# The first three units' y is copied into x by partitions, with the rows of x and w_in in that order; the first v is reversed by a product; some loads begin later

## The chip, the core and the metric

The kernel runs on one core of a Trainium2 chip. The core has five engines that run side by side and meet at semaphores: TensorE (matrix products into PSUM), VectorE (DVE), ScalarE (ACT), GpSimd (POOL) and SyncE (SP), whose queue here does nothing but issue transfers. Transfers between HBM and SBUF, and within SBUF, run on 16 DMA engines that all queues share.

The metric is the device time of one execution in microseconds (us). The time before is a median of 599.5 us over 3 runs (599.27 to 601.45).

## The reference

Two parts are computed one after the other. The first is a recurrence over 768 tokens with a 48 x 48 state per batch and head (4 batches, 8 heads):

```python
f = 1.0 / (1.0 + np.exp(-f_logit))
for t in range(S):
    state = f[:, :, t, :, None] * state + np.einsum('bhd,bhe->bhde', k[:, :, t], v[:, :, t])
    y[:, :, t] = np.einsum('bhd,bhde->bhe', q[:, :, t], state)
```

The second takes y with the heads side by side as x (3072 tokens of 384 values), and is a small network with 2048 hidden values:

```python
h = x @ w_in
g = h * (1.0 / (1.0 + np.exp(-1.702 * h)))
return g @ w_out
```

q, k, v and f_logit arrive as float32. The weights w_in (384 x 2048) and w_out (2048 x 384) arrive as float64 bits, so the kernel turns them into float32 itself.

## The kernel before

**Units.** The 3072 tokens are cut into 12 units of 256. A unit has two halves of 128 tokens (f = 1 is the first, kept in order; f = 0 the second, kept in reversed order), and each half two groups (g) of 64. Eight heads form four pairs (NP); head h of a pair (h = 0 or 1) lies on partitions 64h to 64h+47 (the function `rows`). So of each 64 partitions only 48 hold data.

**The recurrence of a unit** is done in levels. `begin_f`, `begin` and `begin_k` bring the decays F, the queries and the keys to the layout with head dimension on partitions (line 345, or for the first three units, n < N_FILL = 3, products with an identity, line 357, copied out by ScalarE at line 362). `begin_gates` (line 407) multiplies neighbouring decays on POOL into the tile `tot`, level by level (line 413); there is one such tile, so the next unit's gates wait until the last reader of this unit's is done, which is the state update (line 664). Each of six levels l has score products (line 422, `sc`), a `promote` on the DVE that multiplies X by decays (line 516 for the first three units, line 520 for the others), a `set_aside` that copies keys into Kc on ScalarE (line 491) and `evacuate`, which moves the scores under masks into the tile A (lines 463 and 482 on the DVE, 472 on ScalarE). `turn_k` turns the keys (`tkn`, line 592, copied into kn at line 593). The part "S" then makes the products kn with v (`pd`, line 640), `add` makes y from A and v (line 531), and the states st are updated (lines 661 to 665). The last part adds the share of earlier states to y (line 686).

**v** is loaded per unit in two tiles (`load_v`): vt holds the first 128 tokens as they are, vr the second 128 in four transfers of 32 tokens each, in reversed order of the four. `reverse_v` (line 309) turns each 32 rows round by a shuffle on the DVE, so that all 128 stand reversed in vt.

**From y to x.** y lies in PSUM with head dimension on partitions. Eight ScalarE copies per unit (line 698; each of one h, f and g, 48 partitions x 4 pairs x 64 tokens) bring it to the tile yT in SBUF. The function `to_x` then builds xT by transfers: x has 384 rows in three chunks (NK = 3) of 128. Rows 0 to 95 of chunk c are the pair of heads 2c and 2c+1, packed without a gap; rows 96 to 127 of the three chunks together hold the fourth pair. So a unit has two transfers of 48 x 768 (line 737) and four smaller ones of 32 or 16 rows (line 742). w_in is loaded with its rows in the same order, each pair of 128-column blocks as two pieces, 96 and 32 partitions (line 210).

**The network.** h = x w_in is line 1084 for the first four units and o = g w_out line 1098 for the first three; after that the two use schemes with fewer products of smaller blocks, whose operands are sums made on POOL (`sums_of_x`, line 952) and on the DVE. Lines 990 and 853 are their products.

**What sets the order.** For TensorE and POOL the order is that in which the program is written out, everywhere. For the first four units (`opening` and the first `merge` calls, inside `fill_order`) this holds for all engines. After that DVE, ACT and SP are ordered by a planner that goes by estimated times. `opening` is unit 0 with the beginnings of unit 1; `merge` deals the network's products (the list `fill`) between the parts of a unit's recurrence. Weights are fetched by `fetch_weights`, one pair of blocks at a time, three pairs in flight, and turned to float32 by `convert`: one ScalarE operation (line 228) and four DVE operations (lines 230 to 233).

PSUM tiles of the first units come from `bank`, which hands out four lanes in turn, or those in the list `chosen`. A product into a lane waits until the earlier tile there has been read. On SP each transfer waits for the transfer eight places before it, since the program has eight counters for them.

In `opening` unit 0's parts that matter here stand in this order: scores of level 5, the last gelu table, `turn_k`, the copies of the scores into A with v's reversal between them, the queries of unit 1, then part "S" with the keys of unit 1 between pd and y. There, `begin_k` of unit 1 ends with the set-aside copy Kc, and only then come y's products and a 1 x 1 copy of y by ScalarE (`seen`, line 651), for which the next products into y wait.

Of the kernel before, what the change touches and what calls it, by code (L numbers as in the profile page):

```python
# [9 lines left out]
F32 = mybir.dt.float32  # L10
# [3 lines left out]
ALU = mybir.AluOpType  # L14
# [9 lines left out]
def kernel(  # L24
# [137 lines left out]

    q_end = const.tile([P, NP], F32, name="q_end")
# [7 lines left out]
    D2, DR = 2 * D, P - 2 * D  # L171
    assert NP == NK + 1 and NK * DR == D2
# [5 lines left out]
    for r in range(NGR):  # L178
        ffs = range(r * FG, (r + 1) * FG)
        for ff in ffs[::2]:  # L180
            f = slice(ff * P, (ff + 2) * P)
            pairs.append((w_in[:, :, f], [
                (lambda t: t[:D2], moe_w_in[0:NK * D2, f].rearrange("(c p) f -> p c f", c=NK)),
                (lambda t: t[D2:], moe_w_in[NK * D2:DM, f].rearrange("(c p) f -> p c f", c=NK)),
            ]))
        for ff in ffs[::2]:
            pairs.append((w_out[:, ff:ff + 2, :], [
                (lambda t: t[:], moe_w_out[ff * P:(ff + 2) * P, :].rearrange("(c p) f -> p c f", c=2))]))
# [100 lines left out]
    def load_v(n):  # L289


        if n >= NALL:
            return
        b, s0 = n // NU, n % NU * U
        vts[n] = ld.tile([P, 2, DM], F32, tag="vt", name=f"vt_{n}", bufs=2)
        vrs[n] = ld.tile([P, DM], F32, tag="vr", name=f"vr_{n}", bufs=1)
        nc.sync.dma_start(
            out=vts[n][:, 1].rearrange("p (h d) -> p h d", h=H), in_=v[b, :, s0:s0 + HALF, :].rearrange("h p d -> p h d")
        )
        for i in range(4):  # L300
            t0 = s0 + U - 32 * (i + 1)
            nc.sync.dma_start(
                out=vrs[n][32 * i:32 * (i + 1)].rearrange("p (h d) -> p h d", h=H),
                in_=v[b, :, t0:t0 + 32, :].rearrange("h p d -> p h d"),
            )

    def reverse_v(n):

        nc.vector.stream_shuffle(vts[n][:, 0], vrs[n], list(range(31, -1, -1)))
# [9 lines left out]
    def attention(n):  # L319
# [58 lines left out]
        def begin_f(pieces=None):  # L378
# [7 lines left out]
            if n >= N_FILL or (n == 1 and R - 4 in pieces):  # L386
                load_raw(n + 1, 0)
# [6 lines left out]
        def begin_k(between=None):  # L394
# [9 lines left out]
            else:  # L404
                set_aside(0)

        def begin_gates():
            t["tot"], off = att.tile([P, NA], F32, tag="tot", name=f"tot_{n}"), 0
            for m in LEV:
                nb = NA // (2 * m)  # L410
                t2 = t["tms"][-1].rearrange("p (n two) -> p n two", two=2)
                tn = t["tot"][:, off:off + nb]
                nc.gpsimd.tensor_tensor(tn, t2[:, :, 0], t2[:, :, 1], ALU.mult)  # L413
# [214 lines left out]
        def _():  # L628
# [17 lines left out]
            if not n:  # L646
                units[1][0][2]()
                add()

                seen = t["py"][HS:HS + 1, 1, 0, 1, :1]  # L650
                nc.scalar.copy(seen, seen)
            load_v(n + 1)
            st = att.tile([P, NC, NP, D], F32, tag="st", name=f"st_{n}", bufs=2)
# [15 lines left out]
        def _():  # L669
# [22 lines left out]
            if width(n) > U:  # L692
                nc.gpsimd.memset(xT[:, :, U + 1:], 0.0)
            def half(h):
                for f in (1, 0):
# [37 lines left out]
        def to_x(y, x, ng, hs=range(2)):  # L733

            for h in hs:
                most, rest = y(h)
                nc.sync.dma_start(out=x[h * D:(h + 1) * D].rearrange("p c (g t) -> p c g t", g=ng), in_=most)
                at = 0
                while at < D:
                    c, p = (h * D + at) // DR, (h * D + at) % DR  # L740
                    w = min(D - at, DR - p)
                    nc.sync.dma_start(
                        out=x[D2 + p:D2 + p + w, c].rearrange("p (g t) -> p g t", g=ng), in_=rest(h * HS + at, w)
                    )
                    at += w
# [508 lines left out]
    def opening():  # L1254
# [17 lines left out]
        fetch_weights()  # L1272
# [12 lines left out]
        chosen[:] = [2, 3]  # L1285
        turn_k(0)
        turn_k(2)
        for l in range(NL - 1):
            evacuate(l)
            if l == 1:  # L1290
                units[0][3]()
# [64 lines left out]
```

## Time and profile before

| | |
|---|---|
| median of 3 runs | 599.5 us |
| the profiled execution | 599.04 us |
| its span, first to last instruction | 596.9 us |
| mean granted TensorE clock | 0.994 |
| TensorE busy (products) | 574.9 us, 96% |
| VectorE busy | 431.5 us, 72% |
| ScalarE busy | 291.8 us, 49% |
| GpSimd busy | 138.1 us, 23% |
| the eight yT copies of all units (line 698) | 96 copies, 35.3 us |
| transfers yT to xT | 24 of 144 KB, 24 of 32 KB, 24 of 16 KB |

In the page's lists, PE is TensorE's products, PEld its weight loads, which overlap them. A product in float32 appears as two passes, so the counts of the trace are twice those of the program. A row of the timeline gives start, busy time, engine, line, operation and tiles, and in brackets how long the engine had been idle before it and what ended that. A row of the chain of waits gives start, duration and what the time went to; "issue" is time in which an engine waited for nothing that the profile shows. A row of a table of stretches gives the stretch, its length, the busy times of PE, PEld, DVE, ACT and POOL with their instructions, the granted TensorE clock, the share of the DMA engines' time and GB/s.

The span falls into three stages: up to some 75 us units 0 and 1 are begun while the weights arrive; from there to about 560 us recurrence and network are interleaved; the last 37 us finish the last unit.

### The profile page before, as it was taken

To read this page: it belongs to the slowest core of one execution; us is meant where nothing else is said; L and a number is where in the kernel's file an instruction comes from. 1 tells how busy PE (TensorE), PEld (TensorE's weight loads), DVE (VectorE), ACT (ScalarE), POOL (GpSimd) and SP (SyncE) were. 2 spreads that over 40 slices of the span, in tenths; PEclk is the share of its full clock that TensorE was granted. 3 is DMA by queue.
4 is the path that set the end of the run, shared out by engine and by line. 5 is a ranking of instruction groups with operands and counts; after the bars stand their busy time and mean duration, and the time that the engine had idled before them with its cause. 6 is when DMAs were issued, how large, how long until landed. Compare 5 with 4: busy or idle time off the path is not lost.

```text
span 596.9 us, 18468 instructions
## 1 busy us (share of the span) xinstructions
PE 574.9 (96%) x7814; PEld 513.7 (86%) x7814; DVE 431.5 (72%) x696; ACT 291.8 (49%) x613; POOL 138.1 (23%) x214
## 2 busy tenths in 40 slices
PE   6868899999999999999999999999999999999897
PEld 6756776867768789999999999999999999999897
DVE  2898986974866857889777888786887786361284
ACT  4746633453334352574574574573663564552440
POOL 3031200240027216412602502502502503303000
PEclk9979999999999999999999999999999999999999
DMA  7947857950242552353552343552361211001000
GB/s 187 208 124 176 195 143 192 238 110 1 52 106 65 141 136 64 78 132 82 130 147 43 88 113 82 139 133 61 97 158 42 63 37 29 27 3 27 28 1 26
DMA packets 83314, 58.29 MB, mean 98 GB/s; under 512 B 33633, under 2 KB 75265, under 8 KB 83233
## 3 DMA queue, kind: packets, MB, share of 16 engines
q1 hardware_dynamic: 82896, 56.73, 38.5%
q8 instruction: 61, 1.00, 0.7%
q10 hardware_dynamic: 337, 0.39, 0.3%
q14 instruction: 20, 0.16, 0.1%
HBM read 43.98 MB, written 8.39 MB: 88 GB/s over the span
## 4 chain that ended last, share of the span: by engine, by line
PE 76%; DVE 11%; ACT 6%; issue 3%; POOL 2%; DMA 2%; SPq 0%; DVEq 0%; ACTq 0%; POOLq 0%
PE h L990 15%; PE h L1084 13%; PE o_Y L853 9%; PE o L1098 9%; PE o_Z L853 7%; PE h_y L990 6%; PE sc L422 5%; PE o_X L853 3%; PE o_W L853 3%; ACT yT L698 2%; POOL tot L413 2%; PE y L531 1%; PE y L686 1%; DVE g L1018 1%; PE t L357 1%
## 5 line engine op out<-in xcount | busy, mean ns | idle before, releaser
L1084 PE MATMUL h<-xT,w_in 128*128 128x256 f32 x384 | 89.2, 387 | 2.0 <-DMA xT<-yT 1.9
L1084 PEld LDWEIGHTS h<-xT,w_in 128*128 128x128 f32 x384 | 72.7, 193 | 13.9 <-DMA xT<-yT 2.0
L491 ACT COPY Kc<-X 128x512 f32<-128x512 f32 x72 | 48.4, 672 | 72.3 <-DVE X L520 57.5
L520 DVE TENSOR_TENSOR X<-X,tot 128x1024 f32<-128x1024 f32 x45 | 57.5, 1278 | 32.2 <-PE sc L422 22.7
L1098 PE MATMUL o<-w_out,g 128*128 128x384 f32 x192 | 65.5, 491 | 0.4 <-DVE w_out L233 0.4
L413 POOL TENSOR_TENSOR tot<-F 128x512 f32<-128x512 f32 x12 | 12.5, 1041 | 204.5 <-DVE st L664 198.3
L1098 PEld LDWEIGHTS o<-w_out,g 128*128 128x128 f32 x192 | 35.4, 190 | 22.7 <-DVE w_out L233 0.9
L990 PE MATMUL h<-E,w_in 128*128 128x128 f32 (+1 forms) x420 | 53.4, 275 | 0.0
L853 PE MATMUL o_Y<-T,S 128*128 128x192 f32 x288 | 50.6, 329 | 0.0
L990 PEld LDWEIGHTS h<-E,w_in 128*128 128x128 f32 x420 | 50.1, 192 | 0.0
L1020 ACT ACTIVATE g<-g 128x512 f32<-128x512 f32 (+1 forms) x63 | 35.7, 585 | 25.7 <-DVE g L1018 25.2
L1088 ACT ACTIVATE g<-h 128x256 f32<-128x256 f32 x64 | 23.9, 383 | 48.5 <-PE h L1084 48.0
L853 PEld LDWEIGHTS o_Y<-T,S 128*128 128x128 f32 x288 | 46.8, 190 | 0.5
L698 ACT COPY yT<-y 48x256 f32<-48x256 f32 x96 | 35.3, 368 | 21.6 <-PE y L686 20.5
L482 DVE COPY_PREDICATED A<-masks,sc 128x256 f32<-128x256 uint32 (+1 forms) x98 | 42.0, 506 | 0.1
L1018 DVE TENSOR_TENSOR g<-g,h 128x512 f32<-128x512 f32 (+1 forms) x52 | 31.8, 632 | 12.6 <-PE h L990 11.5
L345 DVE STREAM_TRANSPOSE X<-raw 128x512 f32<-128x512 f32 x36 | 38.1, 1107 | 0.1
L372 POOL TENSOR_SCALAR F<-F 128x1024 f32<-128x1024 f32 x10 | 15.2, 1522 | 95.5 <-ACT F L375 83.8
L952 POOL TENSOR_TENSOR E<-xT 128x128 f32<-128x128 f32 (+1 forms) x32 | 19.4, 616 | 73.9 <-DMA xT<-yT 33.5
L422 PEld LDWEIGHTS sc<-X,Kc 48*64 48x64 f32 x1440 | 26.3, 136 | 11.1 <-issue 4.7
L422 PE MATMUL sc<-X,Kc 48*64 48x64 f32 x1440 | 31.1, 222 | 4.8 <-DVE s L230 1.3
L1018 DVE TENSOR_TENSOR g<-g,h_y 128x512 f32<-128x512 f32 (+1 forms) x26 | 16.5, 634 | 21.9 <-PE h_y L990 19.7
(159 smaller groups left out, 1169.3 us busy)
## 6 DMA issues: line engine op xcount, KB each, us to landing
bits<-in_moe_w_out_dram SPq DMA_DIRECT2D x8, 768.0 KB, 7.0
raw<-in_f_logit_dram SPq DMA_DIRECT2D x48, 96.0 KB, 3.1
raw<-in_k_dram SPq DMA_DIRECT2D x48, 96.0 KB, 3.3
bits<-in_moe_w_in_dram SPq DMA_DIRECT2D x8, 576.0 KB
raw<-in_q_dram SPq DMA_DIRECT2D x44, 96.0 KB, 2.3
k_tok<-z SPq DMA_DIRECT2D x56, 64.0 KB, 1.8
kt<-k_tok SPq DMA_DIRECT2D x14, 256.0 KB, 3.2
xT<-yT SPq DMA_DIRECT2D x24, 144.0 KB, 2.9
```

The lines of the kernel that those rows point to most:

```text
L345: nc.vector.transpose(view(out, at, [[HALF, NP], [step, R4], [R4 * step, 32]]), by_half[:, j, f].rearrange("p a (j d) -> p (a j) d", j=R4) ...
L422: nc.tensor.matmul(t["sc"][h][g * HS:(g + 1) * HS, a, s, :], lhsT=t["Kc", l][rows(h), x:x + HS], rhs=rhs(h, a, g), start=True, stop=True,)
L482: moved = nc.vector.copy_predicated(out=view(A, c * HALF + at, dims), mask=mask.bitcast(U32), data=got)
L491: nc.scalar.copy(c.rearrange("p (n two m) -> p n two m", two=2, m=m), view(X, KF * SLOT, [[2 * m, SLOT // (2 * m)], [(KR - KF) * SLOT + m, ...
L520: nc.vector.tensor_tensor(x, x, y, ALU.mult)
L698: nc.scalar.copy(view(yT[rows(h)], at, [[U, NP], [step, HS]]), py[columns(h, g), g, :, f, :])
L853: nc.tensor.matmul(t[name], lhsT=lhs(f), rhs=rhs(f), start=(new and i == 0), stop=(i == HF - 1), skip_group_check=True,)
L990: nc.tensor.matmul(ph[:, t], lhsT=WA[a][:, f * P:(f + 1) * P], rhs=E[n][b], start=(root and t == 0), stop=not goes_on, skip_group_check=True,)
L1018: nc.vector.tensor_tensor(to, to, part, ALU.add if sign > 0 else ALU.subtract)
L1020: nc.scalar.activation(to, to, AF.Gelu_apprx_sigmoid)
L1084: nc.tensor.matmul(ph, lhsT=w_in[:, c, ff * P:(ff + 1) * P], rhs=xTs[n][:, c, :], start=(c == 0), stop=(c == NK - 1))
L1098: nc.tensor.matmul(t["po"], lhsT=g[ff // FG][:, ff % FG, tt * P:(tt + 1) * P], rhs=w_out[:, ff, :], start=(ff == ffs[0]), stop=(ff == ffs[ ...
```

## The change

1. **Rows of x and w_in.** Chunk c of x now has head 2c+h on partitions 64h to 64h+47, exactly where y has it, and partitions 64h+48 to 64h+63 hold 16 rows of the fourth pair. w_in's pieces follow: four per pair of blocks (two of 48, two of 16 partitions) instead of two.
2. **y straight into x** for units 0, 1 and 2: for each h, four ScalarE copies of 48 x 64 bring the fourth pair to yT, from where three transfers of 16 rows each build the rest of x, and four copies of 48 x 192 write the three other pairs from PSUM into xT. In unit 0 the small copies and transfers of both h come before all the larger copies. From unit 3 on, the copies to yT stay as they were, and a unit has two transfers of 48 x 768 and six of 16 rows.
3. **The first v** is loaded in natural order in one transfer, and turned round by a product with a reversed identity (`turned`, made on POOL), which ScalarE copies to vt. It stands before `turn_k` in TensorE's order; the shuffle of unit 0 is gone.
4. **Loads**: the third `fetch_weights` (w_out's first pair) and the load of unit 2's f move from before unit 0's levels and from its level 3 to part "S" of unit 0, behind the loads of unit 1's v.
5. In part "S" of unit 0, y's products and the 1 x 1 copy now stand before the set-aside copy Kc of unit 1.
6. From unit 5 on, the last level of the gates goes into a tile of its own, with two buffers, instead of into `tot`.

```diff
+    turned = const.tile([P, P], F32, name="turned")
+    nc.gpsimd.memset(turned, 0.0)
+    nc.gpsimd.affine_select(
+        out=turned, in_=turned, compare_op=ALU.not_equal, fill=1.0, base=1 - P, pattern=[[1, P]], channel_multiplier=1
+    )
...
-    D2, DR = 2 * D, P - 2 * D
+    D2, DR = 2 * D, HS - D
...
-                (lambda t: t[:D2], moe_w_in[0:NK * D2, f].rearrange("(c p) f -> p c f", c=NK)),
-                (lambda t: t[D2:], moe_w_in[NK * D2:DM, f].rearrange("(c p) f -> p c f", c=NK)),
+                (lambda t, h=h: t[h * HS:h * HS + D], moe_w_in[0:NK * D2, f].rearrange("(c h p) f -> h p c f", c=NK, h=2)[h])
+                for h in range(2)
+            ] + [
+                (lambda t, h=h: t[h * HS + D:(h + 1) * HS],
+                 moe_w_in[NK * D2:DM, f].rearrange("(h c p) f -> h p c f", c=NK, h=2)[h])
+                for h in range(2)
...
+        if n == 0:
+            nc.sync.dma_start(
+                out=vrs[n].rearrange("p (h d) -> p h d", h=H), in_=v[b, :, s0 + HALF:s0 + U, :].rearrange("h p d -> p h d")
+            )
+            return
...
+        if n == 0:
+            pt = bank([P, DM], f"v_{n}")
+            nc.tensor.matmul(pt, lhsT=turned, rhs=vrs[n], start=True, stop=True)
+            nc.scalar.copy(vts[n][:, 0], pt)
+            return
         nc.vector.stream_shuffle(vts[n][:, 0], vrs[n], list(range(31, -1, -1)))
...
-            if n >= N_FILL or (n == 1 and R - 4 in pieces):
+            if n >= N_FILL:
                 load_raw(n + 1, 0)
...
             else:
+                if between:
+                    between()
                 set_aside(0)
...
+                if m == LEV[-1] and n > N_FILL + 1:
+                    tn = att.tile([P, nb], F32, tag="D64", name=f"D64_{n}", bufs=2)
                 nc.gpsimd.tensor_tensor(tn, t2[:, :, 0], t2[:, :, 1], ALU.mult)
...
             if not n:
-                units[1][0][2]()
-                add()
-
-                seen = t["py"][HS:HS + 1, 1, 0, 1, :1]
-                nc.scalar.copy(seen, seen)
+                def values():
+                    add()
+
+                    seen = t["py"][HS:HS + 1, 1, 0, 1, :1]
+                    nc.scalar.copy(seen, seen)
+                units[1][0][2](values)
             load_v(n + 1)
+            if not n:
+                fetch_weights()
+                load_raw(2, 0)
...
+            def copies(h, to, heads):
+                for f in (1, 0):
+                    for g in range(NG):
+                        at, step = (g * HS, 1) if f else (U - 1 - g * HS, -1)
+                        nc.scalar.copy(
+                            view(to, at, [[U, heads.stop - heads.start], [step, HS]]), py[columns(h, g), g, heads, f, :]
+                        )
+
             def half(h):
+                if n < N_FILL:
+                    copies(h, yT[rows(h), NK:], slice(NK, NP))
+                    to_x(lambda h: (None, lambda r, d: yT[r:r + d, NK]), xT[:, :, :U], NG, (h,))
+                    if n == 0 and h == 0:
+                        return
+                    for x in (0, 1) if n == 0 else (h,):
+                        copies(x, xT[rows(x)], slice(0, NK))
+                    return
...
-                nc.sync.dma_start(out=x[h * D:(h + 1) * D].rearrange("p c (g t) -> p c g t", g=ng), in_=most)
-                at = 0
-                while at < D:
-                    c, p = (h * D + at) // DR, (h * D + at) % DR
-                    w = min(D - at, DR - p)
+                if most is not None:
+                    nc.sync.dma_start(out=x[rows(h)].rearrange("p c (g t) -> p c g t", g=ng), in_=most)
+                for c in range(NK):
                     nc.sync.dma_start(
-                        out=x[D2 + p:D2 + p + w, c].rearrange("p (g t) -> p g t", g=ng), in_=rest(h * HS + at, w)
+                        out=x[h * HS + D:(h + 1) * HS, c].rearrange("p (g t) -> p g t", g=ng),
+                        in_=rest(h * HS + c * DR, DR),
                     )
-                    at += w
...
         load_raw(1, 1)
         fetch_weights()
-        fetch_weights()
...
-        chosen[:] = [2, 3]
+        chosen[:] = [2, 3, 2]
+        units[0][3]()
         turn_k(0)
         turn_k(2)
         for l in range(NL - 1):
             evacuate(l)
-            if l == 1:
-                units[0][3]()
```

More of the change, by code (lines that the diff above doesn't have):

```diff
@@ L170 @@
     k_toks = [tc.dram_tile([2, G, P // 32, 32 * NP], F32, name=f"k_tok{j}") for j in range(2)]
[L171 to L172 removed]
+    D2, DR = 2 * D, HS - D
+    assert NP == NK + 1 and NK * DR == D
     NGR = NFF // FG
```

## The prediction

> **What bounds the kernel now.** I read the page's busy times and slices first, then the stretches, then inside the first 130 us the waits of TensorE, the chain of waits and the timeline.
>
> ```profile
> PE 574.9 (96%) x7814; PEld 513.7 (86%) x7814; DVE 431.5 (72%) x696; ACT 291.8 (49%) x613; POOL 138.1 (23%) x214
> PE   6868899999999999999999999999999999999897
> ```
> ```profile
> 70.00:80.00 10.00, 9.39 (x118) 6.62 (x119) 9.86 (x16) 6.14 (x14) 4.75 (x6) 1.00 0.66 132
> 200.00:300.00 100.00, 99.25 (x1374) 92.81 (x1374) 78.79 (x117) 50.39 (x105) 34.98 (x45) 1.00 0.43 107
> 300.00:400.00 100.00, 99.73 (x1428) 97.14 (x1428) 78.71 (x121) 57.03 (x110) 22.68 (x38) 1.00 0.43 107
> ```
>
> The columns of a stretch are its length, then PE, PEld, DVE, ACT, POOL busy. From 200 to 400 us TensorE is idle for 1.0 us: work moved there on another engine can win next to nothing. From 75 to 125 us it is busy for all of 50.0 us. So what counts is when TensorE gets through the first 75 us, and every delay there is carried to the end. Three places in it matter. First the timeline of unit 0 from 22 us:
>
> ```profile
> 21.96 1.09 PE L592 MATMUL tkn<-ident,X 128*128 128x128 f32 x8
> 22.66 1.07 ACT L593 COPY kn<-tkn 128x512 f32<-128x512 f32 x2
> 23.29 1.97 PE L357 MATMUL t<-ident,raw 128*64 128x128 f32 x32 [0.24 <-ACT kn L593]
> 24.47 0.70 DVE L309 STREAM_SHUFFLE vt<-vr 128x384 f32<-128x384 f32 x1
> 27.17 1.51 ACT L472 COPY A<-sc 32x256 f32<-32x256 f32 x4 [0.39 <-DVE A L482]
> 30.07 1.10 PE L531 MATMUL y<-A,vt 64*48 64x64 f32 x62 [1.59 <-ACT X L362]
> ```
>
> The shuffle sits between the DVE's copies into A, but ScalarE waits only 0.39 us for them; the run of ScalarE (kn, X, a, A, X) is almost as long, and TensorE's y waits for its end. Second, the chain of waits at x of unit 0 and at unit 1:
>
> ```profile
> 35.68 0.45 ACT Kc L491
> 36.12 3.26 DMA xT<-yT
> 39.38 0.04 issue
> 39.43 4.39 PE h L1084 x12
> ...
> 73.63 0.36 ACT yT L698
> 73.99 0.02 issue
> 74.02 0.69 ACT Kc L491
> 74.71 0.04 issue
> 74.75 0.70 PE sc L422 x32
> ```
>
> Unit 0's h waits for the transfer yT to xT; unit 1's does not: there the eight yT copies and the Kc copy behind them hold the scores, so copies are the price, not transfers. Third, the clock (the number behind POOL's busy time):
>
> ```profile
> 36.00:37.00 1.00, 0.57 (x20) 0.57 (x24) 0.96 (x2) 0.38 (x1) 0.00 (x0) 0.50 0.32 74
> 41.00:42.00 1.00, 1.00 (x4) 0.82 (x3) 0.86 (x3) 0.00 (x0) 0.00 (x0) 0.50 1.01 390
> 42.00:43.00 1.00, 1.00 (x4) 0.78 (x4) 0.97 (x2) 0.38 (x1) 0.00 (x0) 0.72 1.00 389
> ```
>
> Unit 0's first twelve h matmuls take 4.39 us against 2.86 us for twelve at 71.76: they begin at half clock, which lasts until some 42.6 us.
>
> **The change, part by part.** Times are those of the profiled execution, 599.04 us (span 596.9 and 2.1 around it); the median of the runs shown, 599.5, is 0.46 above it.
>
> *First v by a product.* Gone: 0.70 us of DVE. Added: one fp32 product of 384 columns, two passes of 0.34 (sixteen such o passes take 5.43), so 0.68 us on TensorE ahead of tkn, and a ScalarE copy 128x384 of 0.475 (the sum<-o row, 2.9 for 6) ahead of kn. The second tkn takes the product's bank and waits for that copy. tkn_0 starts at 22.64, the v copy ends about 23.3, tkn_2 runs 23.4 to 24.0, its copy ends 24.65, and t, now in that bank, starts at 24.8 instead of 23.29: +1.5. ScalarE's X, a and A copies follow, less the 0.39 us for which they waited for the DVE: +1.1, and y with them, at 31.2. Bounds: if y is let go by the A copies, not by X, it starts at 29.6 (-0.5); if nothing of the 0.39 comes back, +1.5. I take +1.1, since the 1.59 us row names X. pd moves from 25.19 to 26.7, the state updates behind it by about 0.9, and the DVE's weight conversions likewise; the DVE sits idle for 2.37 us before 46.41, which swallows that.
>
> *seen ahead of Kc.* Kc ended (30.80) before y did (31.19), so nothing was held. Now Kc ends about 0.4 us before the yT copies can start. No gain, no cost.
>
> *y straight into x, unit 0.* Before: 8 copies of 256, 0.38 us apart, and six transfers issued 0.6 us apart from 34.15, the last at 37.33, landing about 39.4, which is 6.9 us after y's end at 32.54. Now 8 copies of 64 and 8 of 192. ScalarE's PSUM copies cost 0.31 at 192 elements, 0.475 at 384: 0.21 at 64. Transfers start after four small copies (0.9), go out every 0.6 with nothing to wait for, the last at 3.9, landing 2.1 later: 6.0 after y's end. But the sixteen copies take 8x0.21 + 8x0.315 = 4.2 instead of 3.04, Kc takes 0.7 more, and the scores of unit 1 (1.13 at half clock) stand ahead of h in TensorE's order: h at 6.25. So h starts at 32.54 + 1.1 + 6.25 = 39.9, +0.47. Until 42.68 it runs at half rate (2.78 us do 1.39 of 2.86), so it ends at 44.15 instead of 43.82: **+0.3**. Ends: -2.2 (h at 38.8 and never cooled) and +2.1 (cold 3.4 us longer).
>
> *The same for unit 1.* Sixteen copies again, 4.2 against 3.04, ahead of Kc. TensorE had finished its h at 74.62 and already waited, so the scores at 74.75 move by **+1.15**, and behind 75 us nothing gives it back. Ends: 0.4 (copies of 64 at 0.12, as the 1x1 copy) to 1.4. The transfers themselves are needed only at 80.65 (h of unit 1); they land about 79.
>
> *Unit 2.* Four copies (1.51) become eight (2.1) ahead of a Kc that waited 0.44 us for the DVE anyway, and the scores that read it stand behind TensorE's o: 0.
>
> *Loads.* On SP, v's reversed load is one issue instead of four (2.06 to 0.5) and q of unit 1 goes out 1.5 us sooner; nobody waited. The second v load now waits for the product (22.7) instead of the shuffle (25.2). Behind it stand w_out's first pair (19.12 to about 24.8, read at 39.20), f of unit 2 (19.85 to 25.2, read at 43.75) and x: covers of 7, 14 and 9 us less 5 to landing. w_in's pieces go from two to four: 16 more issues of 0.45 us. At the start they fit before f's load, for which SP waits until 8.70. The tight place is the pair issued at 41.12 and read at 51.59: its last piece goes out at 42.9 and lands 7.8 us later, 50.7. Cost 0 to 2, taken 0. From unit 3 on x takes eight transfers instead of six: 1.2 us on SP; TensorE waits for none of these transfers behind 100 us.
>
> *POOL.* The matrix for the product: a memset and a select of 0.20 and 0.29 (ident's rows) at 3.2 us; POOL's next work is at 9.45. The last gates in a tile of their own: tot waits for the state updates 198 us in all, but no TensorE wait names POOL. 0; the orders planned for DVE, ACT and SP shift with it, and with 1.3 us of TensorE idle in 300 that is +-1.
>
> Sum +0.3 + 1.15 = +1.45: 600.5 for a profile, **601.0 us** as a median.
>
> *A rule against the change.* The row first: the two pieces of that w_in pair are issued 0.42 us apart and overlap. The Trainium skill, page "DMA: Bandwidth & Descriptors", section "Rules for kernel authors", advises one 128-partition transfer over pieces by partitions, and gives a fixed cost of about 2.0 us each. By it two further pieces, paid one after the other, would be an estimated 4 us and the sum would be 605; by the row they are 0.9 us of issue, hidden.
>
> **The rivals.**
>
> *Longer cold (slower).* Half clock lasted from about 35.8 to 42.6, some 6.8 us, over two gaps of TensorE. If the 3.4 us before its usual end holds too little work because h starts at 39.9 or later, another 3.4 us at half clock follow: the h take 5.7 us and t and scores half more, +2.0 instead of +0.3: 602.7. Against it: scores and h are unbroken from 38.8. It decides from an h start past some 40.5. The Trainium skill, page "TensorE: Matmul & The Clock Gate", Part 1, has full rate return after a busy window of about 3.4 us that runs free; 39.43 to 42.6 in the row is near that.
>
> *The product is hidden (faster).* y starts at 30.07 as before, h at 38.8 with the clock never lowered: 2.86 us from there end 2.2 us sooner; with unit 1's +1.15 that is 598.4. For it: x's transfers are no longer last. Against: the ScalarE run.
>
> *w_in's pieces late (slower).* If the pair read at 51.59 lands after 51.9, ScalarE blocks with X behind it, and the DVE, 97% busy from 50 to 60 us, stands too: 2 us late gives 603.0. Against: a margin of 1.2 us.
>
> **The numbers.** Forecast 0.62, longer cold 0.14, product hidden 0.13, late pieces 0.06, other shifts of the planned orders 0.05. Measurement tells about 0.5% (3.0 us) from no change: 596.5 to 602.5 is the same. Faster needs all of the second rival and 2 us more: 0.04; slower is the two slow rivals, nearly whole, 0.17; same 0.79. The range takes 598.4 less 0.6 of planned orders and 603.0 plus 0.3: 597.8 to 603.3.
>
> **What would show it.** The product near 22.0 and t at 24.8 instead of 23.29; y's start at 31.2; six small transfers from about 34.6; h at 39.9 with its twelve at 4.2 to 4.4 us; TensorE idle for over 1 us before the scores at some 76 us, named Kc. A second cold stretch, h before 39, or a w_in wait on ScalarE would prove me wrong, and so would any new TensorE wait behind 125 us.

## The result

The changed kernel takes 603.03 us as a median of 16 executions (600.15 to 604.61), the kernel before 599.9 us beside it. The two medians are 3.1 us apart; the ratio on record, which is the measure used from here on, is 1.0043 with a 95% interval of 1.0032 to 1.0054, so +2.6 us (+1.9 to +3.2). A second set of 12 executions gave 1.0040 (1.0025 to 1.0055). That is within the 0.5% called "the same", at its upper edge, and inside the range 597.8 to 603.3; the forecast was +1.45.

The profiled execution of after took 603.37 us (span 601.6, clock 0.991), that of before 599.04 (596.9, 0.994). So the two traces differ by 4.7 us in span, more than the medians do; outside its span an execution takes 1.8 us instead of the 2.1 that the prediction kept. Before's trace is about 1 us below the medians of its kernel seen later (599.9 to 600.5), and after's is a little above its own.

The page of after, first the busy time of TensorE, then its share in 40 slices, then the granted clock in the same slices (9 is 90% or more):

```profile
PE 577.3 (96%) x7816; PEld 514.1 (85%) x7816; DVE 429.8 (71%) x694; ACT 295.9 (49%) x638; POOL 135.6 (23%) x216
PE   6978899999999999999999999999999999999897
PEclk9979989999999999999999999999999999999999
```

The sixth slice (75 to 90 us) shows a clock below 0.9, which before does not have there (0.9 or more). The timeline of unit 0 in after, TensorE alone:

```profile
22.30 0.91 PE L326 MATMUL v<-vr,turned 128*128 128x384 f32 x2
25.11 1.97 PE L377 MATMUL t<-ident,raw 128*64 128x128 f32 x32 [0.68 <-ACT kn L618]
29.98 1.11 PE L556 MATMUL y<-A,vt 64*48 64x64 f32 x64
33.16 0.51 PE L447 MATMUL sc<-X,Kc 48*64 48x64 f32 x17 [0.44 <-issue]
37.88 1.14 PE L447 MATMUL sc<-X,Kc 48*64 48x64 f32 x32 [3.48 <-ACT Kc L516]
38.94 4.63 PE L1127 MATMUL h<-xT,w_in 128*128 128x256 f32 x12
```

The product stands where it was expected, and t comes 1.8 us later than in before (23.29). Yet y runs at once at 29.98: the wait of 1.59 us that before had in the middle of y is gone. So unit 0's h ends at 43.57 instead of 43.82, 0.25 us *earlier* than in before. Up to unit 1's y this lead stays. Then the timeline of ScalarE and TensorE around unit 1's y, in after:

```profile
71.18 0.86 ACT L727 COPY yT<-y 48x64 f32<-48x64 f32 x4 [0.99 <-PE y L715]
72.07 1.29 ACT L727 COPY xT<-y 48x192 f32<-48x192 f32 x4
73.37 0.86 ACT L727 COPY yT<-y 48x64 f32<-48x64 f32 x4
74.25 1.28 ACT L727 COPY xT<-y 48x192 f32<-48x192 f32 x4
75.55 0.67 ACT L516 COPY Kc<-X 128x512 f32<-128x512 f32 x1
...
76.28 0.83 PE L447 MATMUL sc<-X,Kc 48*64 48x64 f32 x32 [1.90 <-ACT Kc L516]
77.04 6.93 PE L1141 MATMUL o<-w_out,g 128*128 128x384 f32 x16
```

The same o in the timeline of before:

```profile
75.38 5.43 PE L1098 MATMUL o<-w_out,g 128*128 128x384 f32 x16
```

Sixteen copies take 4.3 us instead of 3.04, Kc and the scores named for it come 1.53 us later, and then the same sixteen o passes take 6.93 us instead of 5.43. The stretches of after tell why (third number from the end of a row is the granted clock):

```profile
75.00:76.00 1.00, 0.00 (x0) 0.00 (x0) 0.56 (x1) 0.96 (x3) 0.63 (x1) 1.00 0.08 17
76.00:77.00 1.00, 0.72 (x32) 0.65 (x32) 0.68 (x1) 1.00 (x4) 0.00 (x0) 0.85 0.09 22
77.00:78.00 1.00, 1.00 (x7) 0.66 (x3) 0.85 (x3) 1.00 (x2) 0.00 (x0) 0.50 0.12 28
79.00:80.00 1.00, 1.00 (x3) 0.57 (x2) 0.45 (x2) 0.00 (x0) 0.00 (x0) 0.50 0.57 181
80.00:81.00 1.00, 1.00 (x4) 0.57 (x4) 0.00 (x0) 0.00 (x0) 0.00 (x0) 0.94 1.01 402
```

TensorE is idle for the whole microsecond from 75, and from 76.7 to 80.1 its clock is half. Unit 1's first h starts at 83.81 instead of 80.65: +3.16 us so far. Two smaller places follow, in the timeline of after (TensorE at unit 2's x; then SP, POOL and TensorE in the last unit):

```profile
134.75 7.11 PE L1127 MATMUL h<-xT,w_in 128*128 128x256 f32 x30 [0.56 <-DMA xT<-yT]
...
547.74 1.86 SPq L785 DMA_DIRECT2D xT<-yT_last  x3
550.97 0.78 POOL L995 TENSOR_TENSOR E<-xT 128x129 f32<-128x129 f32 x2 [19.85 <-DMA xT<-yT_last]
551.44 0.71 PE L1033 MATMUL h<-E,N_c 128*128 128x129 f32 x4 [1.46 <-POOL E L995]
```

The last transfers of before and its first E, in the timeline of before:

```profile
542.85 1.23 SPq L742 DMA_DIRECT2D xT<-yT_last  x2
545.37 0.79 POOL L952 TENSOR_TENSOR E<-xT 128x129 f32<-128x129 f32 x2 [17.15 <-DMA xT<-yT_last]
```

y of the last unit starts 2.9 us later than before, E 5.6 us later: SP issues 16 transfers in 10.6 us (539.01 to 549.60) where it issued 12 in 7.96. TensorE, which waited for no E before, now waits 1.46 us. So the theory to test was: the opening gives a little, unit 1's copies take 1.5, the half clock behind them another 1.5, and SP's four issues in the last unit 1.5.

### The profile page after: what moved, and what is told of

Same layout as the page of the kernel before. It is cut to its first block, busy times and chain, and to the rows that moved or that the text cites. A ratio compares the mean times of both kernels' runs of the same rounds, so it can differ in the third digit from the quotient of the medians.

```text
span 601.6 us, 18560 instructions
## 1 busy us (share of the span) xinstructions
PE 577.3 (96%) x7816; PEld 514.1 (85%) x7816; DVE 429.8 (71%) x694; ACT 295.9 (49%) x638; POOL 135.6 (23%) x216
## 4 chain that ended last, share of the span: by engine, by line
PE 78%; DVE 9%; SPq 3%; DMA 3%; ACT 2%; issue 2%; POOL 1%; ACTq 0%; DVEq 0%; POOLq 0%
PE h L1033 17%; PE h L1127 11%; PE o_Y L896 10%; PE o_Z L896 7%; PE o L1141 6%; PE h_y L1033 6%; PE sc L447 6%; PE o_W L896 3%; PE o_X L896 3%; PE t L377 2%; DVE X L541 2%; SPq L785 1%; PE y L556 1%; PE y L715 1%; PE sc L665 1%
## 5 line engine op out<-in xcount | busy, mean ns | idle before, releaser
L1141 PE MATMUL o<-w_out,g 128*128 128x384 f32 x192 | 67.0, 500 | 0.4 <-DVE w_out L243 0.4
L743 ACT COPY yT<-y 48x256 f32<-48x256 f32 x72 | 26.4, 366 | 19.6 <-PE y L715 18.8
L1052 ACT ACTIVATE g<-h 128x512 f32<-128x512 f32 (+1 forms) x46 | 26.2, 577 | 10.2 <-PE h L1033 10.0
```

Source lines behind the costliest of these rows:

```text
L743: nc.scalar.copy(view(yT[rows(h)], at, [[U, NP], [step, HS]]), py[columns(h, g), g, :, f, :])
L1141: nc.tensor.matmul(t["po"], lhsT=g[ff // FG][:, ff % FG, tt * P:(tt + 1) * P], rhs=w_out[:, ff, :], start=(ff == ffs[0]), stop=(ff == ffs[ ...
```

## The experiments

Each kernel ran in turn with the kernel before on the same chip, and each ratio is against it (0.001 is 0.6 us).

**1. Unit 1's large copies behind Kc.** Base: the changed kernel.

```diff
-                    if n == 0 and h == 0:
+                    if n == 1 or n == 0 and h == 0:
                         return
...
+            if n == 1:
+                return lambda: [copies(h, xT[rows(h)], slice(0, NK)) for h in range(2)]
```

> Edit: unit 1's eight large ScalarE copies of y into x (192 elements each) go behind the Kc copy that the next unit's second level waits for; its small copies and transfers stay ahead. Theory A (the sixteen copies ahead of Kc are the stall, and the half clock that follows the stall is its child): the scores named Kc start at 74.0 to 74.8 instead of 76.28, the twelve-to-sixteen o behind them take 5.4 us instead of 6.93, the first h of unit 1 starts near 80.7, and the time is 2.5 to 3.1 us below the change's 603.0, about 600.0 to 600.5, ratio to the kernel before 1.000 to 1.001. Rival 1 (the cost sits in the opening, the product and its later transposes): at most -0.5, 602.5 or more. Rival 2 (half clock there has to do with the phase of a free running window and not with the stall): the scores come 1.5 us sooner but the half clock stays, -1.5, 601.5.

Measured: 1.0024 (1.0006 to 1.0042), about 1.1 us below the changed kernel, less than half of what was expected. At the place itself all came as theory A has it: the scores start at 74.09, the sixteen o take 5.57, unit 1's h starts at 80.13. But then, in the timeline of this run, ScalarE and TensorE:

```profile
104.10 0.91 ACT L238 ACTIVATE a<-bits 128x768 f32<-128x768 f32 x1 [4.29 <-DMA bits<-in_moe_w_out_dram]
...
105.57 2.86 PE L1129 MATMUL h<-xT,w_in 128*128 128x256 f32 x12 [0.87 <-ACT sum L1193]
109.79 0.66 PE L617 MATMUL tkn<-ident,X 128*128 128x128 f32 x4 [1.36 <-DVE sum L1195]
```

A load of w_out lands at 104.1 (101.8 in before), ScalarE and the DVE stand behind it, and TensorE waits 2.2 us at a place where neither earlier trace has a wait. In the changed kernel's trace SP issues this load at 95.77, here at 98.81, and TensorE comes there 3.7 us later than here. So the stall of unit 1 seems to have hidden a second cost; runs 4, 6 and 7 follow this. The time alone would fit rival 2 as well, but the o ran at full clock.

**2. Warm products in the stall.**

```diff
             scores("y" if l in (2, 4) else "sc")
+            if n == 2 and l == 1:
+                for _ in range(2):
+                    nc.tensor.matmul(
+                        t["sc"][0].rearrange("p a s t -> p (a s t)")[:, :(NL - 1) * 64], lhsT=ident,
+                        rhs=masks.rearrange("p l f t -> p (l f t)"), start=True, stop=True,
+                    )
             score(0, l, queries(l))
```

> Edit: two products that nobody reads (128x320, two passes each) stand on TensorE ahead of the scores that wait for Kc behind unit 1's y; all else is the changed kernel. Theory A (an idle gap of 1.9 us brings the half clock): the wait for Kc stays, the scores still start near 76.3, but no half clock follows and the o behind them take 5.4 instead of 6.9 us: -1.5, 601.5, ratio 1.0025. Rival (the half clock comes from the phase of a window, not from this gap): no change, 603.0 +-0.4, and the products cost up to 0.6 us more where Kc is ready before they end.

Measured: 1.0027 (1.0008 to 1.0046), some 1.0 us below the changed kernel; the interval does not exclude nothing or 1.5. The timeline of this run:

```profile
74.86 1.24 PE L567 MATMUL sc<-masks,ident 128*128 128x320 f32 x4
76.48 0.70 PE L447 MATMUL sc<-X,Kc 48*64 48x64 f32 x32 [0.38 <-ACT Kc L516]
77.11 5.43 PE L1147 MATMUL o<-w_out,g 128*128 128x384 f32 x16
```

The scores come no earlier, but the o run at full clock. The changed kernel was run once more for such comparisons, beside runs 5 to 7:

> The changed kernel once more, beside these on the same chip, so that they are compared with it and not with another day's runs. Both theories: ratio to the kernel before 1.0043 +-0.0015. Theory A (the stall before Kc brings the half clock at 77 us in most executions): a mean clock of 0.991 or less in most, 0.994 or more in few, and those with 0.994 some 1.7 us shorter.

It gave 1.0040 (1.0025 to 1.0055), as said. The granted clock of all executions says more than one trace. Of the changed kernel's 28 executions, 18 have a mean clock of 0.992 or less (in a span of 600 us, 3.4 us at half clock are 0.003); with the copies moved (1) it is 1 of 12, with the warm products 2 of 12. Over all runs of this document, those that leave the gap open (the changed kernel, 3, 5 and 9) have 40 of 56, those with the copies moved (1, 4, 7, 10 and 11) 3 of 60. So the gap brings the half clock, in most executions, not in all. The kernel before, which has no such gap there, has 38 of 108: a mean clock tells how many stretches of 3.4 us ran at half rate (one at 0.997, two at 0.994, three at 0.991 or 0.992, in every trace), not where. For the changed kernel, in its second set, the executions with 0.991 had a median of 603.08, those with 0.994 one of 601.86.

**3. The last token's transfers from ScalarE's queue.**

```diff
-                to_x(lambda h: (yl[rows(h), :NK], lambda r, d: yl[r:r + d, NK]), xT[:, :, U:U + 1], 1)
+                to_x(lambda h: (yl[rows(h), :NK], lambda r, d: yl[r:r + d, NK]), xT[:, :, U:U + 1], 1, engine=nc.scalar)
```

> Edit: the eight transfers of the last token's y into x are issued from ScalarE's queue instead of SP's, whose eight transfers of the last unit stand ahead of them. Theory A (sixteen issues of about 0.64 us on SP instead of twelve make POOL's E late, and the last h wait for it): E starts by 545.5 instead of 550.97, TensorE's wait of 1.46 us for E goes, -1.3 to -1.6, 601.5, ratio 1.0025. Rival (E is late by the landing of the unit's own x transfers, or the wait is only renamed, to DVE or a DMA): 0, 603.0. On the losing side, ScalarE's issues could hold the evacuations of the last o: up to +0.6 a transfer that stands ahead of one, +1 in all.

Measured: 1.0004 (0.9985 to 1.0023), 2.3 us below the changed kernel, somewhat more than expected. The wait for E is gone from TensorE's waits. The timeline of this run:

```profile
76.12 0.70 PE L447 MATMUL sc<-X,Kc 48*64 48x64 f32 x32 [1.47 <-ACT Kc L516]
76.75 5.43 PE L1141 MATMUL o<-w_out,g 128*128 128x384 f32 x16
...
546.09 0.79 POOL L995 TENSOR_TENSOR E<-xT 128x129 f32<-128x129 f32 x2 [16.73 <-DMA xT<-yT_last]
```

Its profiled execution happens to be one without the half clock at 77, though the wait for Kc is there; 10 of its 12 executions have a clock of 0.991 (median 601.17), the two others 0.994 (599.25). This is what a gap that cools TensorE only in some executions would look like.

**4. Both edits together** (1 and 3).

> Edit: the first and the third of these edits together. Theory A: they act at different places and add, -4.0 to -4.7: 598.3 to 599.0, ratio to the kernel before 0.997 to 0.9985. Rival (something else behind takes over when both waits go): -3.0 or less, 600.0, ratio 1.000 or more.

Measured: 0.9992 (0.9974 to 1.0010). Against the changed kernel that is -3.1 us, short of the -4.0 to -4.7: here too TensorE waits at 104 to 110 us (0.8 us for the DVE's sum), and the same load is what ScalarE waits for, 2.6 us. All 12 executions have a clock of 0.993 or more.

**5. The first v by the shuffle again.** Part 3 of the change undone, all else kept.

```diff
-        chosen[:] = [2, 3, 2]
-        units[0][3]()
+        chosen[:] = [2, 3]
         turn_k(0)
         turn_k(2)
         for l in range(NL - 1):
             evacuate(l)
+            if l == 1:
+                units[0][3]()
```

> Edit: the changed kernel with its first v turned as before, by four reversed loads and the DVE's shuffle between the copies into A; all else as in the changed kernel. Theory A (the opening with the product is not slower, the cost is at unit 1 and in the tail): -0.5 to +0.3 from the changed kernel, 602.5 to 603.3, ratio to the kernel before 1.003 to 1.005; unit 1's wait for Kc stays at 1.4 to 1.9 us. Rival (t, 1.8 us later by the product and its banks, is what is carried to the end): -1.1 to -1.8, 601.5, and the scores of unit 1 named Kc 1 us earlier than 76.28.

Measured: 1.0041 (1.0025 to 1.0057), no difference that can be told from the changed kernel. In the trace y of unit 0 runs from 28.66 to 30.23 with no wait (29.98 to 31.09 with the product). Counted from the first product behind the levels (tkn here, v in the changed kernel), y ends after 7.77 us here and 8.79 with the product, and within 0.02 us of these in every trace with the late loads, so the product does cost the opening 1.0 us. The trace also shows where the lead went in this execution, first unit 1's scores and the last unit in the timeline, then its stretches:

```profile
74.77 0.70 PE L432 MATMUL sc<-X,Kc 48*64 48x64 f32 x32 [1.90 <-ACT Kc L501]
...
548.55 0.87 PE L1018 MATMUL h<-E,N_c 128*128 128x129 f32 x4 [1.88 <-POOL E L980]
549.21 2.77 PE L881 MATMUL o_Y<-T,S 128*128 128x192 f32 x8
```

```profile
550.00:552.00 2.00, 2.00 (x9) 2.00 (x8) 0.00 (x0) 0.00 (x0) 1.92 (x5) 0.50 0.00 0
```

The same eight o_Y took 1.47 us in the changed kernel. Here the wait for E, 1.88 us, is the one that is followed by the half clock, and the wait for Kc, again 1.90 us, is not. Even so the span is 1.2 us shorter than the changed kernel's (600.4 against 601.6), yet the two executions take the same (603.43 and 603.37 us). An execution's time less the start of its last transfer in the span is 5.9 us here and 4.6 there; it is 5.8 and 6.1 in the two later runs with the shuffle (10 and 11), 4.6 to 4.7 in every run with the product, and 4.9 in before. So the microsecond that the shuffle gains in the opening is lost again ahead of the first instruction or behind the last transfer. Why is not shown.

**6. Four pieces of w_in in the kernel before.** This was formed from experiment 1: only the pieces are split, rows and the rest stay.

```diff
-                (lambda t: t[:D2], moe_w_in[0:NK * D2, f].rearrange("(c p) f -> p c f", c=NK)),
-                (lambda t: t[D2:], moe_w_in[NK * D2:DM, f].rearrange("(c p) f -> p c f", c=NK)),
+                (lambda t, x=x: t[x:x + D], moe_w_in[0:NK * D2, f].rearrange("(c p) f -> p c f", c=NK)[x:x + D])
+                for x in (0, D)
+            ] + [
+                (lambda t, x=x: t[D2 + x:D2 + x + DR // 2],
+                 moe_w_in[NK * D2:DM, f].rearrange("(c p) f -> p c f", c=NK)[x:x + DR // 2])
+                for x in (0, DR // 2)
```

> Edit: the kernel BEFORE with only this: each of w_in's two pieces by partitions is split in two (48, 48, 16 and 16 partitions), rows and all else as they were. My prediction priced the four pieces at 0. Theory A1 (they cost nothing that TensorE sees): 0 +-0.5 us against the kernel before, ratio 0.999 to 1.001. Theory B, formed from the first experiments (SP comes 0.3 to 1.7 us later to the transfers behind the pieces, and the pair of w_out that is converted at 102 us, whose buffer comes free at 96.3 and which was issued at 96.64, lands later; TensorE then waits for the DVE's sums at 104 to 110 us): ScalarE's wait for w_out's bits grows from 1.5 to 2.5 or more, TensorE waits 0.5 to 2 us between 104 and 110, ratio 1.001 to 1.004.

Measured: 1.0033 (1.0017 to 1.0049), so +2.0 us (1.0 to 2.9). Theory A1, and with it my price of 0, is wrong. The timeline of this run, ScalarE, TensorE and SP:

```profile
102.64 0.90 ACT L232 ACTIVATE a<-bits 128x768 f32<-128x768 f32 x1 [2.54 <-DMA bits<-in_moe_w_out_dram]
...
108.32 0.66 PE L596 MATMUL tkn<-ident,X 128*128 128x128 f32 x4 [0.75 <-DVE sum L1154]
133.31 6.71 PE L1088 MATMUL h<-xT,w_in 128*128 128x256 f32 x30 [1.17 <-DMA xT<-yT]
...
128.56 0.58 SPq L741 DMA_DIRECT2D xT<-yT  x1
```

and SP's same transfer in before:

```profile
125.39 0.58 SPq L737 DMA_DIRECT2D xT<-yT  x1
```

Two places pay: the load at 102 us, and unit 2's x, whose first transfer SP issues 3.2 us later, so that h waits 1.17 us. Together 1.9 us, as measured. It is not the pair with the narrow margin (read at 51.59) that suffers, but what SP issues later: that load, 35 us behind the pieces of 62 us, and x, 31 us behind the pieces of 98 us. SP's own waits show how: each transfer waits for the one eight places before it, and from 97 to 130 us SP's loads wait 3.0 us for w_in's pieces, in before not at all. In the changed kernel's trace only the second place shows (0.56 us at 134.75), and in the trace of its second set not even that; there TensorE is late itself. A sentence on the rule weighed in the prediction: the Trainium skill, "DMA: Bandwidth & Descriptors", section "Rules for kernel authors", prefers one wide transfer to pieces by partitions; the run agrees in direction, and its 2.0 us lie between my 0 and the 4 us that I had estimated from the page's fixed cost. That fixed cost of about 2.0 us stands in the page's section "Anatomy of one DMA — SWDGE (gpsimd) path" and is a fit for transfers issued from GpSimd; these are issued from SP.

**7. k behind the load.** The two edits of 4, and unit 3's eight k loads on SP behind w_out's pair.

```diff
-                    parts[1] = parts[1][0], lambda: (second(), [load_raw(n + 1, j) for j in range(3)])
+                    parts[1] = parts[1][0], lambda: (second(), [load_raw(n + 1, j) for j in range(2)])
+                    third = parts[3][1]
+                    parts[3] = parts[3][0], lambda: (third(), load_raw(n + 1, 2))
```

> Edit: unit 1's large copies behind Kc and the last token's transfers from ScalarE's queue, as before, and the eight loads of unit 3's k go on SP behind the load of w_out's pair instead of ahead of it. Theory B (that pair's load, kept back on SP by the k loads after its buffer came free, gave back part of the gain at 104 to 110 us): it is issued near 94.7 instead of 96.4, ScalarE waits under 1 us for it instead of 2.6, TensorE's 0.8 us wait for the DVE's sum there goes: -0.5 to -1.0 from the run with the two edits alone, ratio 0.9975. k is read at 118 us and lands by 105: free. Rival (TensorE's wait there is the DVE's own load, or the DMA engines serve no more): 0, ratio 0.999 to 1.0.

Measured: 0.9975 (0.9952 to 0.9998), the first version whose whole interval is below the kernel before. The timeline of this run, SP and ScalarE:

```profile
92.46 0.39 SPq L220 DMA_DIRECT2D bits<-in_moe_w_out_dram  x1
...
100.91 0.90 ACT L238 ACTIVATE a<-bits 128x768 f32<-128x768 f32 x1
```

The load goes out at 92.46, earlier than I had said, and ScalarE does not wait for it; no wait of TensorE is left between 100 and 130 us. Just behind, at 132.56, unit 2's h waits 0.97 us for x. Against run 4 the gain is 1.0 us, as expected, but the two intervals overlap.

**8. The side edits alone, on the kernel before** (3 and 7 without the change).

> Edit: the kernel BEFORE with two of the side edits alone, the last token's transfers from ScalarE's queue and unit 3's k loads behind the load of w_out's pair; rows, copies and pieces as before. Theory A and B (these edits repair what the change made late: E and w_out's pair): nothing of size to repair here, ratio 0.9985 to 1.0005. Rival (they help the kernel before as much, so that the gain of the run with all three edits, 0.9975, has nothing to do with the change): 0.9965 to 0.998.

Measured: 0.9998 (0.9981 to 1.0015). They gain nothing measurable there, so the gain in 7 seems to need the change: it would be the change's own, freed of what it had made late. The intervals of 7 and 8 overlap a little, and the third edit of 7, the copies, has no counterpart in before, so this is likely and not proved.

**9. The loads back to their early places.** The changed kernel with part 4 undone.

```diff
-            if not n:
-                fetch_weights()
-                load_raw(2, 0)
...
-            if n >= N_FILL:
+            if n >= N_FILL or (n == 1 and R - 4 in pieces):
                 load_raw(n + 1, 0)
...
         fetch_weights()
+        fetch_weights()
         for l in range(NL):
```

> Edit: the changed kernel with its later loads undone: the third weight pair and f of unit 2 are begun where the kernel before begins them, ahead of the first levels; all else as changed. Theory A (in the kernel before, y of unit 0 was held 1.59 us not by ScalarE's X, which my prediction took from that row, but by what those loads do at 24 to 30 us; the later loads removed it, the product put 0.8 to 1.1 us back): y of unit 0 waits again, 0.8 to 1.6 us between its first matmuls and the rest or ahead of them, it ends at 32 or later instead of 31.1, h of unit 0 at 39.8 or later, and the time is 0.5 to 1.5 us above the changed kernel on the same chip, ratio 1.005 to 1.0065. Rival (that wait was ScalarE's run and the order of its copies): no wait comes back, ratio 1.004 +-0.001.

Measured: 1.0060 (1.0040 to 1.0081), 1.0 to 1.2 us above the changed kernel's two sets, though the intervals overlap. The timeline of this run:

```profile
30.72 0.27 PE L377 MATMUL t<-ident,raw 128*64 128x128 f32 x1 [0.51 <-issue]
30.92 1.11 PE L556 MATMUL y<-A,vt 64*48 64x64 f32 x64
...
34.61 0.50 PE L447 MATMUL sc<-X,Kc 48*64 48x64 f32 x17 [1.01 <-issue]
```

Waits are back, not of before's size and not at the same instructions, and they carry no name. y ends at 32.03 and h starts at 39.83, as theory A said; from v to y's end it is 9.57 us instead of 8.79. Set side by side, the traces agree: in all four kernels with the early loads y of unit 0, or the product just ahead of it, waits 0.5 to 1.6 us, in none of the ten with the late loads; and TensorE loses 0.8 to 2.9 us to "issue" between 24 and 36 us with the early loads, 0 to 0.6 with the late ones (1.2 in one, run 2). So the later loads are worth 0.8 us in this trace and about 1 us in time, and y's 1.59 us in before went with them. ScalarE's X, which the row named, runs just as late in after (29.98 to 31.19) and holds nothing. Run 6, with before's order and early loads, shows it most directly: there X runs from 29.20 to 30.41, and y starts in the middle of it (timeline of run 6):

```profile
29.85 1.10 PE L535 MATMUL y<-A,vt 64*48 64x64 f32 x62 [0.89 <-ACT A L476]
```

**10. The three edits and the shuffle** (7 and 5).

> Edit: unit 1's large copies behind Kc, the last token's transfers from ScalarE's queue, k of unit 3 behind w_out's pair, and the first v by the shuffle as before: what is left of the change is the rows, the copies straight into x, the later loads and the tile of the last gates. Theory A (the product costs the opening 0.8 to 1.0 us, and with the stalls behind it gone the opening carries to the end): y of unit 0 ends near 30.2, h at 38.1, 0.5 to 1.2 us below the run with three edits, ratio 0.9955 to 0.9970. Rival (w_in's four pieces and their queue set the pace at 104 to 134 us, so that an earlier opening is only waited away there): ratio 0.9975, with 0.5 to 1.5 us of TensorE waits between 100 and 135 us.

Measured: 0.9981 (0.9965 to 0.9997): the rival's number; no gain from the shuffle. A place behind takes part of it, as the rival said (timeline of this run, SP and TensorE):

```profile
127.22 3.75 SPq L772 DMA_DIRECT2D xT<-yT  x6
...
131.03 7.05 PE L1114 MATMUL h<-xT,w_in 128*128 128x256 f32 x30 [0.79 <-DMA xT<-yT]
```

ScalarE had the copies done by 125.5. SP comes to the transfers only after eight loads of k for unit 4. But run 7 waits at this place too (0.97 us), and its median span is 0.45 us longer than here (596.9 against 596.45), while its median time outside the span is 0.55 us shorter (1.88 against 2.43): the loss outside the span that run 5 has is here again.

**11. Unit 2's x ahead of those loads.** Base: run 10.

```diff
-            if n >= N_FILL or (n == 1 and 2 == 0):
+            if n > N_FILL or (n == 1 and 2 == 0):
                 load_raw(n + 1, 2)
...
                 if rest:
                     rest()
+                if n == N_FILL:
+                    load_raw(n + 1, 2)
```

> Edit: the run before (three edits and the shuffle) with unit 2's six x transfers ahead of the eight loads of unit 4's k on SP, instead of behind them. Theory B (SP, pushed back by the four pieces of w_in, gets to those transfers at 127.2 where the copies are done by 125.5, and TensorE's h of unit 2 at 131 waits 0.8 us for them): the transfers start near 122.5 to 124, that wait goes, -0.8 us, ratio 0.9965 to 0.9975, and what waits remain between 100 and 135 us are the DVE's 0.5. Rival (the wait is passed on to the k loads, read by unit 4's transposes, or to another place behind): no gain, 0.998 or more.

Measured: 0.9958 (0.9940 to 0.9977), so 2.5 us below the kernel before (1.4 to 3.6). The timeline of this run:

```profile
122.64 4.59 SPq L774 DMA_DIRECT2D xT<-yT  x6
...
130.02 6.17 PE L1116 MATMUL h<-xT,w_in 128*128 128x256 f32 x26
```

h no longer waits. The gain over run 10 is 1.4 us where the trace accounts for 0.8; the intervals overlap, so the rest is not shown to be anything.

## Why the prediction was right or wrong

The time and the class were right, the sum was not, and that the time fell into the range was in part luck. +1.45 was made of two terms. The traces' +4.7 has six: the opening -0.25, unit 1's copies +1.8, the half clock behind them +1.6, unit 2's x +0.5, the planned orders -0.8, E +1.6 to 1.8; and outside the span 0.3 us fell away. Three of the signs that the prediction itself named as proving it wrong came: a second cold stretch, an h before 39 us (38.94), and new TensorE waits behind 125 us.

- **First v by a product (+1.1 to y).** Right in size: 1.0 us against the shuffle (run 5). But y came 0.09 us earlier than in before. The step that failed is "I take +1.1, since the 1.59 us row names X": the row named the engine that ended last before y, and the wait went with loads that no row near it names (run 9); in run 6's trace y does not wait for X.
- **Loads, taken 0.** Wrong on both sides. Beginning them later gains about 1 us, and below 0 I had bounded nothing; w_in's pieces cost 2.0 us in the kernel before (run 6). I had priced the pieces by the one pair whose margin I could see, not by SP's order behind them. "1.2 us on SP; TensorE waits for none of these transfers behind 100 us" failed for the last unit's E (1.46 and 1.82 us in the two traces), and unit 2's x, late behind the pieces, made h wait too (0.56 us in one of the two). That TensorE named no wait there before said nothing on how near the transfer was.
- **seen ahead of Kc, no cost.** Right: after the 1 x 1 copy Kc runs from 31.28 to 32.13, and the first yT copy still waits 0.49 us for y.
- **y straight into x, unit 0 (+0.3).** -0.25 in the traces. The copies, the Kc behind them and the scores ahead of h came as described, h at 38.94 instead of 39.9 only because y was earlier than forecast, and its twelve took 4.63 instead of 4.2 to 4.4.
- **Unit 1 (+1.15).** Right mechanism, the sharpest of the text: the scores named Kc at 76.28, forecast "at some 76". The copies grew by 1.31 us, not 1.15, and y itself ended 0.2 us later behind a short issue gap: +1.53 at the scores, and 1.78 counted from the lead of 0.25.
- **Longer cold.** The mechanism was right and the place wrong. I priced the half clock where TensorE was already cold (unit 0) and not where my own main term made a new gap. Behind the 1.90 us wait it costs 1.6 us in the trace, and it comes in most executions (runs 1, 2, 3).
- **POOL's gates, 0.** The time in which tot waited for the state updates fell from 198 us to 65, and no wait of TensorE appeared or went that names the gates. No run undid this part alone, nor part 5.

The rest of the traces' difference, -0.8 us between 140 and 530 us, goes with the planner's other order: of before's three waits of TensorE for ScalarE's copies of o (osb, 1.1 us in all) one is left (0.5 us), and TensorE is busy 100.00 us of the 100 from 300 us, where before it was 99.73. Which part of the change did it was not tried. It is inside the +-1 of the text.

The terms do not add, and this is the main lesson of the runs: taking unit 1's stall away gave 1.1 us instead of 2.5 to 3.1, since waits on late transfers appeared behind it, and only with SP's order mended did more of the gain appear (runs 4, 7, 11). That these waits are the pieces' cost, hidden until then by the stall, is the reading that fits runs 1, 4, 6 and 7; no run took the pieces out of the changed kernel. What stays open: why the early loads hold up TensorE's issue. In that stretch the DMA engines are at their full share (1.04 to 1.20 of their time between 22 and 28 us in before), and the page counts instruction packets among the DMA queues' (62 and 21 in after), so fetching instructions behind the loads is one reading; but after has 1.39 at 24 to 26 us and no such wait, and no run tried it. Open too is why the runs with the shuffle lose their microsecond outside the part of the execution that the engines' rows show (run 5).

## What to carry to other kernels

A stall that you predict is also a gap for the clock: price what TensorE does in the 3.4 us behind it at half rate, at that very place, as a chance and not as a certainty. A queue that only issues transfers has no busy row that warns: where a change adds issues, follow the queue to the next transfers that somebody reads, also 50 us on, and compare the time of issue with the time at which the data was ready. And when removing a wait gives less than its length, look for the next late thing behind it before giving up the theory; here four such moves on SP and ScalarE (and the shuffle, which by itself gave nothing measurable) turned +0.4% into -0.4%.

## What the runs showed of the hardware

A wait of TensorE of 1.9 us was enough for half clock in some executions and not in others: behind the 1.90 us at 76.28 it came, behind 1.88 us for E in run 5 it did, behind 1.90 us for Kc in the same trace it did not, nor behind 1.82 us for E in the second set of the changed kernel, 1.47 us in run 3's trace and 1.46 us for E in the changed kernel. It lasted about 3.4 us each time. The Trainium skill, "TensorE: Matmul & The Clock Gate", Part 1, has a window that runs free, which fits the chance in it. Its section "Why this matters for your kernels" advises against idle gaps of more than about 3 us; here gaps of 1.9 us were followed by half clock, and the measurement decides.

ScalarE's copies out of PSUM have a large fixed part: 64 elements a partition take 0.215 us (0.86 for four), 192 take 0.32, 256 took 0.38. Splitting a copy of 256 into one of 64 and one of 192 costs 0.16 us each time.

An issue on SP of a transfer within SBUF takes about 0.6 us, whether it moves 48 x 768 or 16 x 256 elements, or one token; ScalarE's queue took 0.63 to 0.79 us each (run 3).
